# The last 64 tokens of every batch as a ninth 512-token block of the MLP beside the attention

## The chip, the cores and the metric

The kernel runs on one core of a Trainium2 chip. The metric is the device time of one execution in microseconds (us); lower is better. The kernel before has a median of 1210.61 us over three runs (1206.44 to 1210.83). Engines are named as in the profile: PE is TensorE (matrix products and transposes), PEld its weight loads, DVE is VectorE, ACT is ScalarE, POOL is GpSimd, SP is the engine that issues most DMAs.

## The reference: attention, then a gated MLP

Eight batches of 8 heads, 576 tokens, head size 64. A token of 64-token block i sees all tokens of blocks up to i. The attention's output, reordered to 4608 tokens of 512 features, goes through a gated MLP with 1536 hidden features:

```python
scores = scale * np.matmul(q, k.transpose(0, 1, 3, 2))
mask = block_i >= block_j
scores = np.where(mask, scores, -1000000000.0)
attn = softmax(scores)                       # exp, sum and division, written out in the reference
x = (attn @ v).transpose(0, 2, 1, 3).reshape(B * S, H * D)
...
gate = 1.0 / (1.0 + np.exp(-(x @ w_gate)))   # w_gate, w_val: 512 x 1536
val = x @ w_val
return (gate * val @ w_out).astype(np.float32)
```

The MLP's weights arrive as 64-bit floats and are converted in the kernel.

## The kernel before, in words

**Products.** A number of a product is split into a high and a low part, both in the reduced type float32r, and each product is made of three matmuls: high by high, high by low, low by high. The 1536 hidden features are 12 blocks f of 128 columns. Stage one, beside the attention, does the first four (F1 = 4); stage two, behind it, does the other eight in two groups of four, over six blocks of 768 tokens each, by a seven-product scheme on 2 by 2 blocks (`unit`, products in L834 with 384 columns, `out_block` at L892).

**Attention.** 32 pairs p of heads, four to a batch. `attend(p)` gives steps: scores and softmax of the four 128-token row blocks ("s": PE scores, DVE row maximum at L372, ACT exp at L375), the 64-token tail ("t"), transposes of the probabilities (L250, copied out by ACT at L350), and the product with v ("AV", in L247) of the pair before. AV's result is scaled by DVE (L486) into `xT`; `finish` (L491) writes its high part (ACT, L493) and low part (POOL, L496) into `XH`, `XL` of the batch, and a copy to the DRAM tensor `xT_d`. All attention steps on PSUM go through a pool of three two-bank tiles (`two_banks`, L254); a step waits until the tile that was used three steps ago is read out.

**The MLP of stage one.** `mlp1(b, bank)` (L556) is a generator that issues one matmul per step. For each f and each half of a batch (TA = 288 tokens), `hidden` (L121) makes 12 matmuls of 288 columns for gate and 12 for value; `glu` (L141) takes the tanh (ACT), multiplies (DVE, L147), writes the high part (ACT, L152) and the low part (POOL, for the last batch DVE, L153). That is 192 hidden matmuls a batch. The first 512 tokens lie in `hH`, `hL`; the last 64 in one half of `hHt`, `hLt`, which two batches share. Then `out_mm` (L130) makes 12 matmuls of 512 columns for each 128 tokens: four tiles for an even batch, five for an odd one, whose fifth is the 64 + 64 last tokens of both batches. ACT evicts them (L584) and writes them to `part_d`. While attention runs, stage one has two banks of its own (`mbank`); behind it, `bank` hands out halves of the two-bank tiles.

**What sets the order.** The step lists FIRST (pairs 0 to 6), TURN (7) and REST (8 to 31) give each attention step a number of ticks, 12 a pair. At AV of pair 4b + 4 the matmuls of `mlp1(b)` are added to `left`, and a rate is set so that KEEP of them are left when the next batch comes (L783, L784):

```python
left += F1 * 48 * NC // 4 + 3 * F1 * (5 if pb % 2 else 4)
rate = (left - KEEP[pb > 0]) / (4 * TICKS)
```

So a tick deals 5 or 5.25 matmuls, in batch 0 3.9, in batch 1 5.7. Scores and AV are ordered behind the matmuls dealt so far; a dealt matmul may move forward by up to three ticks (AHEAD). What is left, and all of batch 7, follows behind the attention (`run(mlp)`, L918). Beyond these constraints a scheduler fixes each engine's order at compile time by its own simulation.

**The transition.** Behind the attention DVE converts the first weights of stage two (`sums_gv`, `split_gv`: W00 and W01 in advance, then W10, W11 and `wo2`). The SBUF pools of stage two lie over those of stage one: in order from the end that is freed first, `x0` (features of the even batches), `w1` (gate and value weights of stage one, f = 0 first), `x1` (odd batches) and `m1` (all else of stage one). A tile of stage two is written when the tiles under it have been read for the last time.

Of the kernel before, what the change touches and what calls it, by code (L numbers as in the profile page):

```python
# [40 lines left out]
def attn_glu_kernel(ctx: ExitStack, tc: tile.TileContext, q, k, v, w_gate, w_val, w_out, out):  # L41
# [88 lines left out]
    def out_mm(ps, hH, hL, wo, nf, t):  # L130
        n = 3 * nf
        i = 0
        for f in range(nf):
            for lh, rh in ((hH, wo[:, f, 0]), (hL, wo[:, f, 0]), (hH, wo[:, f, 1])):
                mm = nc.tensor.matmul(ps, lhsT=lh[:, f, t * P:(t + 1) * P], rhs=rh, start=(i == 0), stop=(i == n - 1))  # L135
                i += 1
                yield mm.ins
# [3 lines left out]
    def glu(pool, pg, pv, dst, n, lower):  # L141
# [9 lines left out]
        for cols, hH, hL in dst:  # L151
            nc.scalar.copy(out=hH, in_=h2[:, cols])  # L152
            lower.tensor_sub(out=hL, in0=h2[:, cols], in1=hH.bitcast(F32))  # L153
# [7 lines left out]
    with ExitStack() as s2:  # L161
# [14 lines left out]
        def x_tiles(b):  # L176

            i = b % 2
            if i not in X:
                X[i] = [(xp1 if i else xp0).tile([P, NC, S], F32R, name=f"X{e}{i}") for e in "HL"]  # L180
            return X[i]
# [75 lines left out]
        spare = []  # L257

        def bank():
            if not spare:  # L260
                t = two_banks()
                spare.extend((t[:, 1], t[:, 0]))
            return spare.pop()
# [72 lines left out]
        def attend(p):  # L336
# [154 lines left out]
            def finish():  # L491
                XH, XL = x_tiles(b)
                nc.scalar.copy(out=XH[:, hp], in_=xT)  # L493
                nc.scalar.dma_start(
                    out=xT_d[b, hp * P:(hp + 1) * P, :], in_=xT)
                nc.gpsimd.tensor_sub(out=XL[:, hp], in0=xT, in1=XH[:, hp].bitcast(F32))  # L496
# [58 lines left out]

        def mlp1(b, bank):  # L556
            if not H1:
                H1.extend(mp.tile([P, F1, n], F32R, name=x) for n, x in ((512, "hH"), (512, "hL"), (P, "hHt"), (P, "hLt")))
            hH, hL, hHt, hLt = H1
            XH, XL = x_tiles(b)  # L560
            lo = 64 * (b % 2)
            if b == B - 1:
                ahead.extend(first_sums)
            for f in range(F1):
                convert_until(0, 2 * f + 2)
                for sub in range(2):
                    r = slice(sub * TA, (sub + 1) * TA)
                    pg = bank()
                    yield from hidden(pg[:, :TA], wg[f], XH[:, :, r], XL[:, :, r])
                    pv = bank()  # L570
                    yield from hidden(pv[:, :TA], wv[f], XH[:, :, r], XL[:, :, r])
                    if sub == 0:
                        dst = [(slice(0, TA), hH[:, f, :TA], hL[:, f, :TA])]
                    else:
                        dst = [(slice(0, 512 - TA), hH[:, f, TA:], hL[:, f, TA:]),
                               (slice(512 - TA, TA), hHt[:, f, lo:lo + 64], hLt[:, f, lo:lo + 64])]
                    glu(mp, pg, pv, dst, TA, nc.vector if b == B - 1 else nc.gpsimd)
            convert_until(1, F1)
            wo = W_out[0]
            for t in range(5 if b % 2 else 4):  # L580
                po = bank()
                yield from out_mm(po, *((hH, hL, wo, F1, t) if t < 4 else (hHt, hLt, wo, F1, 0)))
                ost = mp.tile([P, DM], F32, name="ost", bufs=2)
                nc.scalar.mul(out=ost, in_=po, mul=0.5)  # L584
                if t < 4:
                    r = b * S + t * P
                    nc.scalar.dma_start(out=part_d[r:r + P, :], in_=ost)
                else:
                    for j in range(2):
                        r = (b - 1 + j) * S + 512  # L590
                        nc.scalar.dma_start(out=part_d[r:r + 64, :], in_=ost[64 * j:64 * j + 64, :])

# [172 lines left out]
        for p in range(n + 1):  # L771
# [4 lines left out]
            for what, places in (FIRST if p < N_FIRST else TURN if p == N_FIRST else REST):  # L776
                if what.startswith(("AV", "TR")):
                    if prev:
                        prev(what.lower() if what == "AV" else what.lower()[:2] + what[2:])
                    if prev and what == "AV" and pairs[p - 1][1] == NP - 1:  # L780
                        pb = pairs[p - 1][0]
                        mlp = itertools.chain(mlp, mlp1(pb, mbank if p < n else bank))
                        left += F1 * 48 * NC // 4 + 3 * F1 * (5 if pb % 2 else 4)  # L783
# [134 lines left out]
        run(mlp)  # L918
        s1.close()
# [105 lines left out]
```

## Time and profile before

| | |
|---|---|
| median of three runs | 1210.61 us |
| the profiled execution | 1211.92 us, its span 1210.1 us |
| PE busy | 1167.7 us, 96% |
| DVE, ACT, POOL busy | 770.4, 627.7, 332.6 us |
| attention and stage one | up to about 641 us |
| stage two | from about 641 us |

A row of a group names line, engine, operation, output and inputs, shape and count; behind the bar stand busy time, the mean of one, and the engine's idle time ahead of them with what ended it. A row of the timeline starts with the start and the duration in us, and has idle time ahead of it in brackets. Matmuls are pipelined: one takes longer than the distance to the next, so the cost of a row of matmuls is read from start to start.

### The profile page before, as it was taken

Reading aid. Unit: us, or ns where it says so; the run is one execution under the profiler, and the core shown is the slowest. Engines: PE = TensorE matmul, PEld = TensorE weight load, DVE = VectorE, ACT = ScalarE, POOL = GpSimd, SP = SyncE. Lnnn points to the kernel's source line nnn. Section 1 sums busy time; section 2 is a strip of 40 time slices with the busy share of each in tenths; the row PEclk is TensorE's granted clock in tenths of the full one; section 3 lists DMA queues with packets and bytes.
Section 4 is the critical chain, followed back from the end, with each engine's and each line's share of the span. In section 5 each row is a group of like instructions: output and inputs, shape, how many; then the busy total and the mean of one; then the engine's idle time right before and its main releaser. Section 6 shows DMA issues by size and latency. Waiting matters only on the chain.

```text
span 1210.1 us, 20754 instructions
## 1 busy us (share of the span) xinstructions
PE 1167.7 (96%) x7421; PEld 1025.6 (85%) x7421; DVE 770.4 (64%) x1447; ACT 627.7 (52%) x1459; POOL 332.6 (27%) x411
## 2 busy tenths in 40 slices
PE   6989899999999999999999999999999999999996
PEld 3557789888888988888789889999999999998895
DVE  5678945356454545544899976866866655755743
ACT  6776857576676666666444453453454432422420
POOL 0123223133231331322101223123122153262331
PEclk8999999999999999999999999999999999999998
DMA  8664343543544443444243335235287154164153
GB/s 179 168 150 98 97 114 74 118 87 78 118 88 105 99 102 83 98 111 120 91 129 115 106 135 200 72 129 200 59 300 288 59 179 165 55 198 155 55 157 105
DMA packets 249112, 152.52 MB, mean 126 GB/s; under 512 B 189489, under 2 KB 209969, under 8 KB 248369
## 3 DMA queue, kind: packets, MB, share of 16 engines
q1 hardware_dynamic: 237952, 132.02, 39.5%
q10 hardware_dynamic: 11056, 19.17, 4.5%
q8 instruction: 58, 0.95, 0.3%
q14 instruction: 46, 0.37, 0.1%
HBM read 103.81 MB, written 47.33 MB: 125 GB/s over the span
## 4 chain that ended last, share of the span: by engine, by line
PE 73%; DVE 12%; DMA 6%; ACT 3%; POOL 2%; issue 2%; SPq 1%; POOLq 0%; DVEq 0%; ACTq 0%
PE b L834 19%; PE m L126 13%; PE bank L247 13%; PE m L892 9%; PE m L135 6%; PE bank L250 5%; PE b L892 5%; DMA pr<-part_d 3%; DVE XL L724 2%; POOL pr L907 1%; ACT P L375 1%; DMA XB<-xT_d 1%; DVE nm L372 1%; PE m L250 1%; PE bank L126 1%
## 5 line engine op out<-in xcount | busy, mean ns | idle before, releaser
L834 PE MATMUL b<-XH,w 128*128 128x384 f32 x1344 | 352.3, 337 | 5.0 <-DVE v L870 2.5
L834 PEld LDWEIGHTS b<-XH,w 128*128 128x128 f32 x1344 | 244.9, 188 | 12.4 <-DVE v L870 5.3
L834 PE MATMUL b<-XL,w 128*128 128x384 f32 x672 | 225.2, 336 | 0.0
L375 ACT ACTIVATE P<-bank,nm 128x512 f32<-128x512 f32 (+3 forms) x256 | 133.5, 538 | 69.7 <-DVE nm L372 59.0
L834 PEld LDWEIGHTS b<-XL,w 128*128 128x128 f32 x672 | 126.6, 188 | 1.3
L892 PE MATMUL m<-wo,hH 128*128 128x512 f32 x384 | 124.9, 391 | 0.0
L372 DVE TENSOR_REDUCE nm<-bank 128x2 f32<-128x1024 f32 (+3 forms) x128 | 105.0, 820 | 29.4 <-ACT P L375 26.8
L350 ACT COPY G<-bank 128x768 f32<-128x768 f32 (+3 forms) x140 | 93.2, 696 | 29.6 <-PE bank L250 26.2
L126 PE MATMUL m<-XH,wv 128*128 128x288 f32 x448 | 104.2, 304 | 1.7 <-DVE h L147 1.7
L126 PE MATMUL m<-XH,wg 128*128 128x288 f32 x448 | 104.2, 303 | 0.0
L247 PE MATMUL bank<-G,VS 128*64 128x320 f32 (+4 forms) x896 | 98.2, 361 | 0.0
L153 POOL TENSOR_TENSOR hL<-h,hH 128x288 fp32r<-128x288 f32 (+1 forms) x56 | 42.4, 757 | 199.6 <-ACT hH L152 190.7
L907 POOL TENSOR_TENSOR pr<-pr,pr 128x512 f32<-128x512 f32 x36 | 48.0, 1333 | 162.1 <-DMA pr<-part_d 139.5
L247 PEld LDWEIGHTS bank<-G,VS 128*64 128x64 f32 x896 | 55.9, 137 | 36.9 <-issue 3.5
L723 ACT CAST XH<-XB 128x1536 fp32r<-128x1536 f32 (+2 forms) x72 | 66.1, 938 | 34.6 <-DVE XB L721 25.1
L892 PEld LDWEIGHTS m<-wo,hH 128*128 128x128 f32 x384 | 71.9, 188 | 13.7
L857 ACT ACTIVATE g<-g 128x384 f32<-128x384 f32 x72 | 37.4, 524 | 81.6 <-DVE g L870 61.1
L724 DVE TENSOR_TENSOR XL<-XB,XH 128x1536 fp32r<-128x1536 f32 (+2 forms) x72 | 77.8, 1089 | 0.9 <-ACT XH L723 0.4
L126 PEld LDWEIGHTS m<-XH,wv 128*128 128x128 f32 x448 | 74.7, 188 | 4.0 <-DVE h L147 1.9
L392 DVE MEMSET bank<- 64x128 f32 x64 | 10.6, 165 | 105.8 <-PE bank L247 105.2
L126 PEld LDWEIGHTS m<-XH,wg 128*128 128x128 f32 x448 | 74.9, 188 | 3.2 <-issue 1.8
L250 PE MATMUL bank<-ident,P 128*128 128x128 f32 x560 | 75.4, 273 | 0.8 <-DVE rT L419 0.7
(179 smaller groups left out, 2488.4 us busy)
## 6 DMA issues: line engine op xcount, KB each, us to landing
pr<-part_d SPq DMA_DIRECT2D x72, 256.0 KB
xT_d<-xT ACTq DMA_DIRECT2D x32, 288.0 KB
XB<-xT_d SPq DMA_DIRECT2D x16, 576.0 KB
part_d<-ost SPq DMA_DIRECT2D x36, 256.0 KB
out_dram<-ost SPq DMA_DIRECT2D x36, 256.0 KB
VS<-in_v_dram SPq DMA_DIRECT2D x64, 128.0 KB
part_d<-ost ACTq DMA_DIRECT2D x32, 256.0 KB
rqk<-in_k_dram SPq DMA_DIRECT2D x108, 72.0 KB
```

Of the source, the lines that this page charges most:

```text
L126: mm = nc.tensor.matmul(ps, lhsT=lh, rhs=rh, start=(i == 0), stop=(i == n - 1))
L135: mm = nc.tensor.matmul(ps, lhsT=lh[:, f, t * P:(t + 1) * P], rhs=rh, start=(i == 0), stop=(i == n - 1))
L247: pe_last[:] = [nc.tensor.matmul(*args, **kw).ins]
L250: pe_last[:] = [nc.tensor.transpose(*args).ins]
L350: mark("ACT", nc.scalar.copy(out=dst, in_=src))
L372: mark("DVE", nc.vector.tensor_reduce(out=nm[:, c0:c0 + 2], in_=ps[:, :, c:c + n], axis=AX.X, op=ALU.max, negate=True))
L375: mark("ACT", nc.scalar.activation(out=Pi[:, h], in_=ps[:, h, c:c + n], func=AF.Exp, bias=nm[:, c0 + h:c0 + h + 1], accum_out=sm[:, 5 * h ...
L723: nc.scalar.copy(out=XO[j][0][:, a:b], in_=x)
L724: sub = nc.vector.tensor_sub(out=XO[j][1][:, a:b], in0=x, in1=XO[j][0][:, a:b].bitcast(F32))
L834: mm = nc.tensor.matmul(ps, lhsT=lh, rhs=rh, start=(first and k == 0), stop=(k == n - 1), skip_group_check=not first)
L892: mm = nc.tensor.matmul(po[t], lhsT=lh[:, f, t * P:(t + 1) * P], rhs=rh, start=(half == 0 and i == 0), stop=(half == 1 and i == 5))
L907: nc.gpsimd.tensor_add(out=pr[0], in0=pr[0], in1=pr[1])
```

## The change

Stage one takes 512 tokens of a batch in one product of 512 columns: 24 hidden matmuls per f, 96 a batch, and 48 for the output. The last 64 tokens of the eight batches become a ninth block, `mlp1(8)`, which runs behind batch 7, so behind the attention. Its features are made by `tail_x`: four DMAs read the last 64 tokens of batches 0 to 6 from `xT_d` into the low tile of the even batches, ACT rounds the high part, POOL subtracts, and POOL copies those of batch 7 from the odd batches' tiles. The even batches' tiles now lie in `x1` and the odd ones' in `x0`. `hHt` and `hLt` are gone, the tiles of `glu` are 512 wide. Behind the attention, `bank` alternates between halves of two-bank tiles and the two banks of stage one, the output is made two tiles at a time, with the last f of both at the end, and DVE makes the low parts for both last blocks. The ninth block's output is written by POOL's DMA queue. `left` counts 96 + 48 a batch; KEEP stays.

```diff
--- before.py
+++ after.py
@@ -127,13 +127,11 @@
                 i += 1
                 yield mm.ins
-    def out_mm(ps, hH, hL, wo, nf, t):
-        n = 3 * nf
-        i = 0
-        for f in range(nf):
-            for lh, rh in ((hH, wo[:, f, 0]), (hL, wo[:, f, 0]), (hH, wo[:, f, 1])):
-                mm = nc.tensor.matmul(ps, lhsT=lh[:, f, t * P:(t + 1) * P], rhs=rh, start=(i == 0), stop=(i == n - 1))
-                i += 1
+    def out_mm(ps, hH, hL, wo, t, fs):
+        for f in fs:
+            for i, (lh, rh) in enumerate(((hH, wo[:, f, 0]), (hL, wo[:, f, 0]), (hH, wo[:, f, 1]))):
+                mm = nc.tensor.matmul(ps, lhsT=lh[:, f, t * P:(t + 1) * P], rhs=rh, start=(f == i == 0),
+                                      stop=(f == F1 - 1 and i == 2))
                 yield mm.ins
     ahead = []
@@ -148,9 +146,9 @@
         for ins in ahead:
             behind(mul.ins, ins)
         ahead.clear()
-        for cols, hH, hL in dst:
-            nc.scalar.copy(out=hH, in_=h2[:, cols])
-            lower.tensor_sub(out=hL, in0=h2[:, cols], in1=hH.bitcast(F32))
+        hH, hL = dst
+        nc.scalar.copy(out=hH, in_=h2)
+        lower.tensor_sub(out=hL, in0=h2, in1=hH.bitcast(F32))
     def run(gen):
         for _ in gen:
@@ -177,7 +175,7 @@
             i = b % 2
             if i not in X:
-                X[i] = [(xp1 if i else xp0).tile([P, NC, S], F32R, name=f"X{e}{i}") for e in "HL"]
+                X[i] = [(xp0 if i else xp1).tile([P, NC, S], F32R, name=f"X{e}{i}") for e in "HL"]
             return X[i]
@@ -254,13 +252,11 @@
         def two_banks():
             return ps_a.tile([P, 2, 512], F32, name="bank")
-        spare = []
+        turns = itertools.cycle((1, 1, 0))
         def bank():
-            if not spare:
-                t = two_banks()
-                spare.extend((t[:, 1], t[:, 0]))
-            return spare.pop()
+            return two_banks()[:, 0] if next(turns) else mbank()
         def mbank():
             return ps_m.tile([P, 512], F32, name="m")
@@ -490,7 +486,9 @@
             def finish():
                 XH, XL = x_tiles(b)
-                nc.scalar.copy(out=XH[:, hp], in_=xT)
+                cut = nc.scalar.copy(out=XH[:, hp], in_=xT)
+                if p == len(pairs) - 1:
+                    mark("ACT", cut)
                 nc.scalar.dma_start(
                     out=xT_d[b, hp * P:(hp + 1) * P, :], in_=xT)
                 nc.gpsimd.tensor_sub(out=XL[:, hp], in0=xT, in1=XH[:, hp].bitcast(F32))
@@ -553,49 +551,60 @@
         H1 = []
+        NM = 4 * P
+        def tail_x():
+            XH, XL = x_tiles(B)
+            XH1, XL1 = x_tiles(B - 1)
+            done = (B - 1) * D
+            for c in range(NC):
+                src = xT_d[0:B - 1, c * P:(c + 1) * P, NM:S].rearrange("b p s -> p b s")
+                nc.sync.dma_start(out=XL[:, c, :done].rearrange("p (b s) -> p b s", s=D).bitcast(F32), in_=src)
+            x = XL[:, :, :done].bitcast(F32)
+            cut = nc.scalar.copy(out=XH[:, :, :done], in_=x)
+            behind(cut.ins, last["ACT"])
+            nc.gpsimd.tensor_sub(out=XL[:, :, :done], in0=x, in1=XH[:, :, :done].bitcast(F32))
+            for dst, src in ((XH, XH1), (XL, XL1)):
+                nc.gpsimd.tensor_copy(out=dst[:, :, done:NM], in_=src[:, :, NM:S])
         def mlp1(b, bank):
             if not H1:
-                H1.extend(mp.tile([P, F1, n], F32R, name=x) for n, x in ((512, "hH"), (512, "hL"), (P, "hHt"), (P, "hLt")))
-            hH, hL, hHt, hLt = H1
+                H1.extend(mp.tile([P, F1, NM], F32R, name=x) for x in ("hH", "hL"))
+            hH, hL = H1
+            if b == B:
+                tail_x()
             XH, XL = x_tiles(b)
-            lo = 64 * (b % 2)
             if b == B - 1:
                 ahead.extend(first_sums)
             for f in range(F1):
                 convert_until(0, 2 * f + 2)
-                for sub in range(2):
-                    r = slice(sub * TA, (sub + 1) * TA)
-                    pg = bank()
-                    yield from hidden(pg[:, :TA], wg[f], XH[:, :, r], XL[:, :, r])
-                    pv = bank()
-                    yield from hidden(pv[:, :TA], wv[f], XH[:, :, r], XL[:, :, r])
-                    if sub == 0:
-                        dst = [(slice(0, TA), hH[:, f, :TA], hL[:, f, :TA])]
-                    else:
-                        dst = [(slice(0, 512 - TA), hH[:, f, TA:], hL[:, f, TA:]),
-                               (slice(512 - TA, TA), hHt[:, f, lo:lo + 64], hLt[:, f, lo:lo + 64])]
-                    glu(mp, pg, pv, dst, TA, nc.vector if b == B - 1 else nc.gpsimd)
+                pg = bank()
+                yield from hidden(pg, wg[f], XH[:, :, :NM], XL[:, :, :NM])
+                pv = bank()
+                yield from hidden(pv, wv[f], XH[:, :, :NM], XL[:, :, :NM])
+                glu(mp, pg, pv, (hH[:, f], hL[:, f]), NM, nc.vector if b >= B - 1 else nc.gpsimd)
             convert_until(1, F1)
             wo = W_out[0]
-            for t in range(5 if b % 2 else 4):
-                po = bank()
-                yield from out_mm(po, *((hH, hL, wo, F1, t) if t < 4 else (hHt, hLt, wo, F1, 0)))
-                ost = mp.tile([P, DM], F32, name="ost", bufs=2)
-                nc.scalar.mul(out=ost, in_=po, mul=0.5)
-                if t < 4:
+            step = 2 if b >= B - 1 else 1
+            for t in range(4):
+                if t % step == 0:
+                    po = {u: bank() for u in range(t, t + step)}
+                    for fs in ((range(F1 - 1), range(F1 - 1, F1)) if step > 1 else ()):
+                        for u in po:
+                            yield from out_mm(po[u], hH, hL, wo, u, fs)
+                if step == 1:
+                    yield from out_mm(po[t], hH, hL, wo, t, range(F1))
+                ost = mp.tile([P, DM], F32, name="t" if b == B and t > 1 else "ost", bufs=2)
+                nc.scalar.mul(out=ost, in_=po[t], mul=0.5)
+                if b < B:
                     r = b * S + t * P
                     nc.scalar.dma_start(out=part_d[r:r + P, :], in_=ost)
                 else:
                     for j in range(2):
-                        r = (b - 1 + j) * S + 512
-                        nc.scalar.dma_start(out=part_d[r:r + 64, :], in_=ost[64 * j:64 * j + 64, :])
+                        r = (2 * t + j) * S + NM
+                        nc.gpsimd.dma_start(out=part_d[r:r + 64, :], in_=ost[64 * j:64 * j + 64, :])
         W_OF = {1: 0, 5: 1, 2: 2, 4: 3, 7: 4, 6: 5, 3: 6}
         X_OF = {1: 0, 7: 1, 2: 2, 3: 3, 5: 4, 6: 5, 4: 6}
@@ -780,7 +789,7 @@
                     if prev and what == "AV" and pairs[p - 1][1] == NP - 1:
                         pb = pairs[p - 1][0]
                         mlp = itertools.chain(mlp, mlp1(pb, mbank if p < n else bank))
-                        left += F1 * 48 * NC // 4 + 3 * F1 * (5 if pb % 2 else 4)
+                        left += F1 * 6 * NC + 3 * F1 * 4
                         rate = (left - KEEP[pb > 0]) / (4 * TICKS)
                 elif what in "kq":
                     next(pr, None)
@@ -916,6 +925,7 @@
             sums = sums_gv(*e, alone=done)
         x_split(early_x, sums)
         run(mlp)
+        run(mlp1(B, bank))
         s1.close()
         for u in units[1:]:
             wp[u] = pool(f"w{u[0]}{u[1]}")
```

## The prediction

> **What bounds the kernel now.** I read the page first (busy shares, slices), then the windows by stage, then the timeline of PE around the transition.
>
> ```profile
> span 1210.1 us, 20754 instructions
> PE 1167.7 (96%) x7421; PEld 1025.6 (85%) x7421; DVE 770.4 (64%) x1447; ACT 627.7 (52%) x1459; POOL 332.6 (27%) x411
> ...
> PE   6989899999999999999999999999999999999996
> ```
>
> PE is the bound nearly everywhere. The windows (busy us of PE, PEld, DVE, ACT, POOL, then granted clock, DMA share, GB/s) say where it is not:
>
> ```profile
> 74.60:144.73 70.13, 63.53 (x462) 49.53 (x463) 59.05 (x112) 48.98 (x130) 18.89 (x24) 1.00 0.46 111
> 144.73:570.50 425.77, 425.70 (x3307) 370.53 (x3307) 219.03 (x444) 279.12 (x740) 125.86 (x208) 1.00 0.43 99
> 588.60:641.70 53.10, 50.57 (x301) 45.59 (x300) 50.35 (x106) 22.66 (x45) 3.17 (x3) 1.00 0.36 120
> 641.70:671.50 29.80, 27.59 (x157) 26.63 (x155) 29.55 (x58) 16.78 (x29) 5.50 (x4) 0.99 0.34 106
> 671.50:707.50 36.00, 36.00 (x176) 33.03 (x177) 33.52 (x54) 14.48 (x27) 10.89 (x9) 0.96 0.41 140
> ```
>
> The second row is the attention from AV of pair 7, which is issued in pair 8, to that of pair 30: PE has no idle, DVE works half the time, ACT two thirds. The first row, where batch 0's MLP begins, has 6.6 us of PE idle beside a DVE busy for 84%. The third and fourth are the transition: DVE is busy 95% and 99%, PE loses 4.7 us. So in most of the attention a matmul saved is time saved; in the first row it mostly isn't; in the transition more PE work costs its own length less the idle that it fills.
>
> **The prices.** Rows of PE's timeline, the first and last of a run without a break. From 612.00 to 615.16 lie 24 matmuls of 288 columns: 131.7 ns each. From 626.28 to 632.65 lie 28 of 512 columns: 227.5 ns each.
>
> ```profile
> 612.00 0.29 PE L126 MATMUL bank<-XH,wg 128*128 128x288 f32 x1
> ...
> 615.16 0.30 PE L126 MATMUL bank<-XH,wg 128*128 128x288 f32 x1
> ...
> 626.28 0.39 PE L135 MATMUL bank<-wo,hH 128*128 128x512 f32 x1
> ...
> 632.65 0.39 PE L135 MATMUL bank<-wo,hL 128*128 128x512 f32 x1
> ```
>
> Between attention steps, 18 of 288 columns lie from 476.54 to 478.94 (133.3 ns), and runs of 10 and 12 of 512 in the chain take 232 and 228 ns; I take 230.
>
> ```profile
> 476.54 0.43 PE L126 MATMUL m<-XH,wg 128*128 128x288 f32 x2
> ...
> 478.94 0.43 PE L126 MATMUL m<-XH,wv 128*128 128x288 f32 x2
> ```
> ```profile
> 306.16 2.32 PE m L135 x10
> ...
> 437.99 2.74 PE m L135 x12
> ```
>
> The columns of the hidden products are the same before and after: 1536 x 288 = 864 x 512. 1536 matmuls cost 1536 x 0.1317 = 202.3 us, 864 cost 864 x 0.2275 = 196.6 us. So the wider product alone is worth 5.7 us of PE, no more. The Trainium skill ("TensorE: Matmul & The Clock Gate", Back-to-back issue gap) gives N/2.4 + 2.5 ns a matmul: 122.5 and 215.8 ns, by which it would be worth an estimated 1.7 us. The rows here lie above both, by 9 and 12 ns, and I go by them.
>
> **Part by part, stage by stage.**
>
> First, the stretch up to AV in pair 8. Batch 0 deals all but KEEP = 52 of its matmuls there: 188 of 288 columns before (188 x 0.1333 = 25.1 us), 92 of 512 after (21.2 us). PE has less to do by 3.9 us, beside a busy DVE. Bounds 0 and -3.9; the window's 6.6 us of idle says nearer to 0: **-0.5 us**.
>
> Second, pairs 8 to 31. From AV in pair 8 to AV in pair 32 there are 24 x 12 - 4 = 284 ticks (pair 32 deals none ahead of its AV). Before, 52 are left at both ends, so 1152 hidden and 324 output matmuls run: 1152 x 0.1333 + 324 x 0.230 = 153.6 + 74.5 = 228.1 us. After, the rates are 3.4 for batch 1 and 3 a tick for the others, 44 are left at the end, and 52 + 6 x 144 - 44 = 872 run, all of 512: 200.6 us. PE is the bound, so **-27.5 us**. Most of that is the last 64 tokens leaving.
>
> Third, behind the attention, up to stage two. Before: 4 + 192 hidden and 48 + 60 output matmuls, 196 x 0.1317 + 108 x 0.2275 = 50.4 us, in the window's 53.1. After: 44 left, batch 7's 144 and the ninth block's 144: 332 x 0.2275 = 75.5 us: **+25.1 us**.
>
> Fourth, idle of PE in the transition. These rows carry it: waits of 1.28, 1.24 and 2.02 us; 12 matmuls from 671.47 to 675.05 that take 3.58 us, where 12 of a steady run (16.50 us for 95) take 2.08; two hitches of 0.4 and 0.3 us against the 0.51 us that two such matmuls take at 641.84. Together 6.7 us.
>
> ```profile
> 619.80 0.40 PE L126 MATMUL bank<-XH,wg 128*128 128x288 f32 x1 [1.28 <-DVE h L147]
> ...
> 638.59 0.50 PE L135 MATMUL bank<-wo,hH 128*128 128x512 f32 x1 [1.24 <-ACT ost L584]
> ...
> 641.84 0.51 PE L834 MATMUL b<-XH,w 128*128 128x384 f32 x2
> ...
> 642.36 0.91 PE L834 MATMUL b<-XH,w 128*128 128x384 f32 x2
> ...
> 667.73 0.84 PE L834 MATMUL b<-XH,w 128*128 128x384 f32 x2
> ...
> 671.47 0.69 PE L834 MATMUL b<-XH,w 128*128 128x384 f32 x1 [2.02 <-DVE g L870]
> ...
> 675.05 0.40 PE L892 MATMUL m<-wo,hH 128*128 128x512 f32 x1
> ```
> ```profile
> 743.78 16.50 PE b L834 x95
> ```
>
> After, PE has 75.5 us of stage one in which DVE, whose list grows by one block's glu alone, gets ahead; `bank` then has five slots of one product each, so the first to be reused are two f behind, 11 us. I take 6.0 of the 6.7 as gone (bounds: none, and all): **-6.0 us**.
>
> What else is moved is hidden. The ninth block's features: four DMAs on SP, at worst behind the 15.10 us of weight loads below; the nearest landing of such a read is 7.42 us; ACT's cut of 1792 columns is 1.7 us by 1.48 for 1536; POOL's subtraction 4.7 us by 1511 ns for 576. That is 29 us against 332 - 144 = 188 matmuls, 42.8 us, ahead of the block. POOL, which gets this and eight output DMAs, sat idle for 62 us there. The cut waits in ACT's queue for the DMAs; behind it stand batch 7's tanh and casts, and PE misses those only when all five slots are full, 11 us later. The DMAs wait for the last hidden product of batch 6, and none of these is left behind the last AV (the 44 are output products).
>
> ```profile
> 583.77 15.10 SPq L643 DMA_DIRECT2D raw<-in_moe_w_val_dram  x4
> ```
> ```profile
> 568.45 7.42 DMA XB<-xT_d
> ```
> ```profile
> L496 POOL TENSOR_TENSOR XL<-xT,XH 128x576 fp32r<-128x576 f32 x32 | 48.4, 1511 | 58.0 <-ACT XH L493 56.1
> ...
> L723 ACT CAST XH<-XB 128x1536 fp32r<-128x1536 f32 x24 | 34.9, 1476 | 9.2 <-PE b L834 8.1 <-PE m L135 1.0
> ```
> ```profile
> 655.70 1.85 POOL L842 TENSOR_TENSOR hL<-t,hH 128x384 fp32r<-128x384 f32 x1 [62.23 <-ACT hH L841]
> ```
>
> The ninth block reads `w1` longer, and W10 and W11 lie over it. Before, DVE ends W10 and W11 from 634.76 and 649.19 on, 46 and 61 us behind the last AV (588.6).
>
> ```profile
> 634.76 2.10 DVE L679 TENSOR_TENSOR w<-cT,w 128x896 fp32r<-128x896 f32 x2 [1.85 <-ACT w L678]
> ...
> 649.19 2.10 DVE L679 TENSOR_TENSOR w<-cT,w 128x896 fp32r<-128x896 f32 x2 [0.22 <-ACT w L678]
> ```
>
> After, its hidden matmuls are over at 42.8 + 96 x 0.2275 = 64.6 us; if DVE waits for all of them, W10 is there at 67 and W11, 14 us behind as now, at 81. PE needs W10 at 75.5 + two units of 42 x 0.174 = 7.3 us, 90, and W11 at 97. Nothing waits. Stage two behind this is untouched.
>
> Sum: -0.5 - 27.5 + 25.1 - 6.0 = **-8.9 us**. The profiled execution took 1211.9 us, so 1203.0; the median shown is 1.3 us lower than that execution, so **1201.7 us**.
>
> **The rivals.**
>
> *The softmax chain becomes the bound (slower).* AV is ordered behind the matmuls dealt between scores and AV, 20 or 21 before, 12 after, and needs the bank that ACT's second exp group frees.
>
> ```profile
> 475.99 0.39 PE L247 MATMUL bank<-KQ 64*128 64x128 f32 x4
> ...
> 479.20 0.30 PE L247 MATMUL bank<-KH,QBH 128*128 128x288 f32 x1
> ...
> 480.08 1.30 PE L247 MATMUL bank<-G,VS 128*64 128x320 f32 x8
> ```
> ```profile
> 479.26 0.21 ACT L375 ACTIVATION_READ_ACCUMULATOR P<-bank,nm 128x1 f32 x1
> ```
> ```profile
> L584 ACT ACTIVATE ost<-m 128x512 f32<-128x512 f32 x31 | 18.8, 605 | 8.4 <-PE m L135 8.1
> ```
>
> Here the bank is free at 479.47 and AV starts at 480.08. After, from 476.30 (the scores' end): 12 x 0.230, 0.1 for the change of operands and the 0.88 of the tail's scores give 480.04, about the same, since 12 wide matmuls last as long as 20 narrow ones. But ACT's ops of glu, 512 wide, cost 0.6 us (the eviction's row). One ahead of that exp brings it to 480.08, two to 480.68: 0.64 us of wait in each of 24 pairs is 15.4 us, 1218.4 on the profiled execution, 1217.1 as a median. From 0.37 us a pair on the change gains nothing. For it: the margin of one op. Against: ACT's work per f falls (one tanh and one cut, where there were two and six), so two in one place should be rare. Chance 0.13.
>
> *The idle in the transition is not won back* (a wait for the space under W10, or SP held by a read of `part_d` rows that are now written last). Then the first three terms are left, -2.9 us: 1209.0, or 1207.7 as a median; no change. For it: DVE at 95 to 99% in two windows, and tiles that are freed later. Against: the margins of 23 and 16 us above. Chance 0.22.
>
> *Hidden products of 512 columns run worse than output products of 512.* At 4 ns more, the distance of the two 512 rates above (228 and 232), 864 x 0.004 = 3.5 us of the gain are lost: 1205.2. No row shows a hidden product of 512; weights and columns come from the same kinds of tile as the output's. Chance 0.1. The Trainium skill's rule above would leave out an estimated 4.0 us and come to much the same time.
>
> **How the numbers follow.** My forecast has 0.55. About 0.5%, 6 us, is what a measurement of this kernel can tell from no change: faster is below 1204.6, slower above 1216.7. The forecast's own range is 1196 (all idle and the whole 3.9 us won) to 1205. Faster: nearly all of the forecast and a little of the third and second rivals, 0.62; slower: most of the first, 0.11; the rest, 0.27, within. The range starts 1.7 us lower, at 1194 (872 matmuls at 228 instead of 230 ns), and ends at 1212, between the second rival and the first, which leaves out most of the first.
>
> **What would show it.** Right: AVs a steady 17.3 us apart (425.77 / 23 - 27.5 / 24), where the starts below are 16.8 and 20.6 us apart; hidden 512 products at 228 to 231 ns; stage two begins some 4 us earlier than at 641.5 and PE's idle up to the second k is under 1 us. Wrong: idle or a gap ahead of AV or the tail's scores with ACT exp as releaser; waits of PE for `w` or `XH` of the ninth block; L834's first rows later than 641.
>
> ```profile
> 244.28 2.86 PE bank L247 x28
> 261.05 2.86 PE bank L247 x28
> ...
> 442.44 2.86 PE bank L247 x28
> ...
> 463.06 2.86 PE bank L247 x28
> ```

## The result and the profile after

| | before | after |
|---|---|---|
| median | 1210.63 us (4 runs, 1206.44 to 1210.83) | 1195.19 us (4 runs, 1194.74 to 1197.00) |
| profiled execution, its span | 1211.92, 1210.1 us | 1194.74, 1193.0 us |

The ratio is 0.9883, with a 95% interval of 0.9860 to 0.9907: 15.4 us faster, where 8.9 were forecast. The 1195.2 us lie just below the forecast's own range (1196 to 1205) and inside the wider one (1194 to 1212). Both kernels were profiled a second time, so that a stage's difference can be held against how well it repeats. The stages are cut at rows of PE: start of AV in the step of pair 8, last matmul of the last AV, first product of stage two, last matmul.

| stage, us | before | before, second | after | after, second | change (first profiles) | forecast |
|---|---|---|---|---|---|---|
| up to AV in pair 8 | 144.7 | 145.9 | 140.7 | 140.8 | -4.0 | -0.5 |
| to the last AV | 443.7 | 443.5 | 414.2 | 414.3 | -29.5 | -27.5 |
| to stage two | 53.1 | 53.0 | 73.6 | 73.6 | +20.5 | +22.6 |
| stage two | 558.6 | 558.7 | 555.2 | 556.9 | -3.4 | -3.5 |
| sum | 1200.1 | 1201.1 | 1183.8 | 1185.6 | -16.3 | -8.9 |

The rest of the spans' 17.1 us, 0.8, lies behind the last matmul. (The 6.0 us of idle of the forecast are put where they lay: the waits of 1.28 and 1.24 us ahead of stage two, 25.1 - 2.5 = 22.6, and the other 3.5 in it.) The two middle stages repeat within 0.2 us, the outer two within 1.3 and 1.7. For the first stage two profiles show too little: six more kernels below, with the changed kernel's products up to there (`noswap` with the features in other tiles), reach AV in pair 8 at 140.1 to 142.8 us. The least distance from before, 144.7 to 142.8, is still more than the 0.5 of the forecast, but its size is known to some 2 us only.

First the page of the changed kernel: PE is a little busier in its share, with 672 matmuls fewer.

```profile
span 1193.0 us, 19280 instructions
PE 1160.0 (97%) x6749; PEld 976.8 (82%) x6749; DVE 774.3 (65%) x1415; ACT 619.7 (52%) x1372; POOL 320.4 (27%) x366
...
PE   6998999999999999999999999999999999999996
```

Then its windows by stage (busy us of PE, PEld, DVE, ACT, POOL, clock, DMA share, GB/s), which answer to the five of before.

```profile
74.60:140.70 66.10, 60.77 (x375) 40.80 (x375) 57.53 (x107) 46.45 (x117) 17.93 (x18) 1.00 0.49 118
```
```profile
140.70:549.84 409.14, 409.14 (x2788) 324.00 (x2787) 224.81 (x438) 275.95 (x687) 115.63 (x163) 1.00 0.44 104
554.93:628.50 73.57, 73.57 (x329) 60.76 (x326) 60.41 (x106) 28.27 (x43) 7.71 (x5) 1.00 0.28 94
628.50:658.00 29.50, 27.34 (x158) 26.99 (x156) 28.08 (x55) 16.95 (x29) 8.35 (x12) 0.99 0.40 125
658.00:694.00 36.00, 36.00 (x176) 33.03 (x177) 31.04 (x50) 12.57 (x24) 10.53 (x9) 0.96 0.49 166
```

PE has no idle at all from AV of pair 8 to stage two, 73.57 of 73.57 us behind the attention, where it had lost 2.5. DVE is busy 82% there instead of 95%. The start of stage two still has 2.2 us of idle, and DVE is still full there (28.08 of 29.50).

AV is now evenly spaced: its starts in PE's timeline lie 17.08 us apart from pair 12 to pair 31 (17.3 in the mean from pair 8 on, the forecast's figure), where they swung between 16.7 and 21.6.

```profile
231.08 2.93 PE L245 MATMUL bank<-G,VS 128*64 128x320 f32 x28
...
248.16 2.93 PE L245 MATMUL bank<-G,VS 128*64 128x320 f32 x28
...
265.24 2.93 PE L245 MATMUL bank<-G,VS 128*64 128x320 f32 x28
```

The hidden product of 512 columns, which no row of before showed: nine in 2.08 us in the attention, 231 ns each; behind it 12 in 2.72 us, 226.7 ns.

```profile
244.74 0.63 PE L126 MATMUL m<-XH,wg 128*128 128x512 f32 x2
...
246.82 0.62 PE L126 MATMUL m<-XH,wv 128*128 128x512 f32 x2
```
```profile
595.88 0.39 PE L126 MATMUL bank<-XH,wg 128*128 128x512 f32 x1
...
598.60 0.39 PE L126 MATMUL m<-XH,wg 128*128 128x512 f32 x1
```

The ninth block's features and the weights that lie over `w1`, in the timelines of ACT, POOL and DVE:

```profile
557.43 1.70 ACT L565 CAST XH<-XL 128x1792 fp32r<-128x1792 f32 x1 [0.64 <-DMA XL<-xT_d]
```
```profile
559.82 4.52 POOL L567 TENSOR_TENSOR XL<-XL,XH 128x1792 fp32r<-128x1792 f32 x1
```
```profile
618.52 2.09 DVE L688 TENSOR_TENSOR w<-cT,w 128x896 fp32r<-128x896 f32 x2
...
634.24 1.09 DVE L688 TENSOR_TENSOR w<-cT,w 128x896 fp32r<-128x896 f32 x1 [1.13 <-ACT w L687]
...
635.72 1.08 DVE L688 TENSOR_TENSOR w<-cT,w 128x896 fp32r<-128x896 f32 x1
...
649.10 1.20 DVE L702 TENSOR_TENSOR wo<-cT,wo 128x512 fp32r<-128x512 f32 x1
```

The features are ready at 564.3, and PE comes to the ninth block at 595.88, so they are hidden. W10 and W11 are done 65.7 and 81.9 us behind the last AV (554.93), against 67 and 81 in the forecast. PE waits for neither.

The start of stage two in PE's timeline, in the first and the second profile of the same changed kernel, and the rows of DVE ahead of the first:

```profile
657.90 0.69 PE L843 MATMUL b<-XH,w 128*128 128x384 f32 x1 [2.16 <-DVE g L879]
```
```profile
654.49 0.95 DVE L733 TENSOR_TENSOR XL<-XB,XH 128x768 fp32r<-128x768 f32 x1
...
656.42 0.95 DVE L733 TENSOR_TENSOR XL<-XB,XH 128x768 fp32r<-128x768 f32 x1
657.29 0.55 DVE L879 TENSOR_TENSOR g<-b,g 128x384 f32<-128x384 f32 x1
```
```profile
658.25 0.44 PE L843 MATMUL b<-XH,w 128*128 128x384 f32 x1 [2.38 <-DVE g L879]
```

So the wait of 2.02 us of before has stayed: PE needs a bank that the sum at 657.29 reads, and that sum stands in DVE's queue behind conversions of the output's weights and the low parts of the next features (L733). In the first profile the 12 matmuls behind the wait take 3.6 us (661.54 - 657.90), in the second 2.2.

Last, PE's waits from the first output of stage two to the end (us in total, times, longest), of before and of the changed kernel's second profile; the first profile of the changed kernel has none.

```profile
PE b L834 <- DVE v L870: 2.5, 6, 1.1
```
```profile
PE b L843 <- ACT ost L910: 1.7, 1, 1.7
PE b L843 <- DVE g L879: 0.2, 1, 0.2
```

### The profile page after: what moved, and what is told of

Read it like the earlier page. It is cut to its first block, busy times and chain, and to the rows that moved or that the text cites. A ratio compares the mean times of both kernels' runs of the same rounds, so it can differ in the third digit from the quotient of the medians.

```text
span 1193.0 us, 19280 instructions
## 1 busy us (share of the span) xinstructions
PE 1160.0 (97%) x6749; PEld 976.8 (82%) x6749; DVE 774.3 (65%) x1415; ACT 619.7 (52%) x1372; POOL 320.4 (27%) x366
## 4 chain that ended last, share of the span: by engine, by line
PE 83%; DVE 7%; ACT 3%; DMA 3%; issue 1%; POOL 1%; SPq 1%; POOLq 0%; DVEq 0%; ACTq 0%
PE b L843 23%; PE bank L245 13%; PE m L126 13%; PE m L901 10%; PE m L133 8%; PE bank L248 5%; PE b L901 5%; PE bank L126 3%; ACT P L371 2%; DMA pr<-part_d 1%; PE m L248 1%; DVE XL L733 1%; PE bank L133 1%; POOL pr L916 1%; ACT G L346 1%
## 5 line engine op out<-in xcount | busy, mean ns | idle before, releaser
L901 PE MATMUL m<-wo,hH 128*128 128x512 f32 x384 | 124.9, 391 | 0.0
L133 PE MATMUL m<-wo,hH 128*128 128x512 f32 x256 | 84.9, 397 | 0.0
L126 PE MATMUL m<-XH,wv 128*128 128x512 f32 x240 | 82.4, 401 | 0.0
L126 PE MATMUL m<-XH,wg 128*128 128x512 f32 x240 | 82.2, 399 | 0.0
L733 DVE TENSOR_TENSOR XL<-XB,XH 128x1536 fp32r<-128x1536 f32 (+2 forms) x72 | 77.7, 1085 | 0.1
L901 PE MATMUL m<-wo,hL 128*128 128x512 f32 x192 | 75.2, 392 | 0.0
L248 PEld LDWEIGHTS bank<-ident,P 128*128 128x128 f32 x560 | 66.0, 141 | 11.3 <-ACT G L346 0.7
```

The costliest lines, as they stand in the source:

```text
L126: mm = nc.tensor.matmul(ps, lhsT=lh, rhs=rh, start=(i == 0), stop=(i == n - 1))
L248: pe_last[:] = [nc.tensor.transpose(*args).ins]
L733: sub = nc.vector.tensor_sub(out=XO[j][1][:, a:b], in0=x, in1=XO[j][0][:, a:b].bitcast(F32))
L901: mm = nc.tensor.matmul(po[t], lhsT=lh[:, f, t * P:(t + 1) * P], rhs=rh, start=(half == 0 and i == 0), stop=(half == 1 and i == 5))
```

## The experiments

Theory: the gain is the output work and the rows of PE that leave the attention, where PE has no idle. Rivals: the wide product in itself; the rules on banks, output order and tiles that came with it. All kernels but `keep80` and the two repeats are edits of the changed kernel, whose 1195.2 us they are held against; times are medians, ratios are to the kernel before, run beside them. Its medians there were 1208.3 to 1209.5, beside the changed kernel 1210.6, so a distance of some 2 us from 1195.2 says nothing by itself.

**The width alone.** Each hidden product as two halves of 256 columns, dealt together:

```python
ops = [(w[:, c, a], x[:, c]) for c in range(NC) for a, x in ((0, xH), (0, xL), (1, xH))]
for h in range(2):
    r = slice(256 * h, 256 * h + 256)
    for i, (lh, rh) in enumerate(ops):
        mm = nc.tensor.matmul(ps[:, r], lhsT=lh, rhs=rh[:, r], start=(i == 0), stop=(i == n - 1))
        if i % 2:
            yield mm.ins
```

> The changed kernel with each hidden product made as two halves of 256 columns into the same bank; blocks, glu, dealing by ticks and the ninth block stay. Theory (the matmul's fixed cost is the gain): a matmul takes its columns plus about 12 ns, so 256 columns take 118 ns, 1728 of them 204 us where 864 of 512 take 196.6: about 8 us slower than the changed kernel, some 1203 us. Rival (the gain is in the longer product groups and in fewer, larger glu operations, that is in waits): no change, within 1 us. A third outcome: weight loads bound the narrow products, then they take over 130 ns and it is over 20 us slower.

1214.96 us, ratio 1.0050 [1.0032, 1.0068]: about 20 us more than the changed kernel, and more than either expectation. Two rows of PE, 24 matmuls apart:

```profile
607.16 0.28 PE L127 MATMUL bank<-XH,wg 128*128 128x256 f32 x1
...
610.03 0.28 PE L127 MATMUL bank<-XH,wv 128*128 128x256 f32 x1
```

2.87 us, 120 ns each, so two halves cost 12.5 ns more than one whole, and 864 of them 10.8 us. The stages show +10.0 up to the last AV, +3.7 behind it, -1.1 ahead and +7.0 in stage two. The first two hold the price of the halves: 771 products of the changed kernel lie in these stages, 9.6 of the 13.7 us. PE shows no wait in either, so the other 4 us are slower matmuls, and why is open. The last comes with another order of stage two (below), with more waits there, and was in no expectation.

**The ninth block or not.** Products of 512, but the tails of two batches as a 128-token block beside the attention; the features stay in the tiles of before, and `h2` has one buffer:

```diff
+                for f in range(F1):
+                    pt = bank()
+                    yield from hidden(pt[:, :P], wg[f], *XT)
+                    yield from hidden(pt[:, P:2 * P], wv[f], *XT)
...
-        run(mlp1(B, bank))
```

> The 512-column products without the ninth block: the last 64 tokens of each two batches make a 128-token block of their own behind the odd batch's output, beside the attention, with 128-column hidden products (feature tiles laid out as before, one buffer for the product of glu instead of two). Theory (it pays only because the tails are gathered into one 512-column block): 384 narrow products at 65 ns (128 columns plus 12 ns) to 109 ns (the distance of the 128-column transposes) cost 25 to 42 us where the ninth block's hidden products cost 21.8, and the idle behind the attention stays: 1203 to 1225 us, nearer to the upper end. Rival (512 columns alone are the gain): as fast as the changed kernel, about 1195.

1227.2 us, ratio 1.0149 [1.0119, 1.0179], slightly above the theory's upper end. The rows say why a narrow tail is dear:

```profile
644.36 0.28 PE L126 MATMUL bank<-XTH,wv 128*128 128x128 f32 x1
...
645.59 0.27 PE L126 MATMUL bank<-XTH,wv 128*128 128x128 f32 x1
```

Eleven in 1.23 us: 112 ns for 128 columns, half the price of 512. Four such blocks are 384 x 0.112 + 48 x 0.230 = 54.0 us, the ninth block is 144 x 0.2275 = 32.8. The attention and what lies behind it took 24.7 us longer (454.6 and 57.9), 3.0 of it in waits of PE. So gathering all eight tails is worth some 21 us, and the change needs both its parts: wide products with tails in pairs lose 17.7 us to the kernel before. Not all of these 17.7 need be the tails' doing: this kernel also has one buffer for `h2`, and 8.4 us of its distance to the changed kernel lie ahead of pair 8 and in stage two.

**Banks and the order of the output.** Both rules of before behind the attention, then each alone:

```diff
-            return two_banks()[:, 0] if next(turns) else mbank()
+            if not spare:
+                t = two_banks()
+                spare.extend((t[:, 1], t[:, 0]))
+            return spare.pop()
...
-            step = 2 if b >= B - 1 else 1
+            step = 1
```

> The changed kernel with the old handing out of banks behind the attention (both halves of a two-bank tile, three tiles) and with the output one tile at a time. Theory (the ninth block's mass of work covers the waits): at most 1 us slower. Rival (the waits of 1.3 and 1.2 us behind the attention went because of the five slots and the late last f): 2.5 us slower or more, with waits of PE for DVE's product of glu and for ACT's eviction.

> The changed kernel with only the old handing-out of banks (a list of the two halves of a two-bank tile, none of stage one's two banks); the output still two tiles at a time. The run with both old rules was 7 us slower than the change: 5.9 us of it between the last AV and stage two, 1 us in stage two. Theory: the banks carry it, since three two-bank tiles that come free only as pairs make PE wait for the evictions: 5 to 6 us longer behind the attention than the change's 73.6 us, about 1201 us in all. Rival: the order of the output's products carries it, the banks nothing: 73.6 us behind the attention and 1195 to 1196 us in all.

> The changed kernel with only the output of the last two blocks made one tile at a time, as in the rest; the banks as in the change. Theory (the banks carry the 7 us): at most 1 us longer behind the attention, 1195 to 1197 us. Rival (the order of the output carries it): the first output products of a block wait for the last f's high and low parts, one gap of 2 to 3 us for each of the two blocks, so 4 to 6 us longer behind the attention and 1200 to 1202 us.

Both rules: 1202.11, ratio 0.9946 [0.9929, 0.9963], 79.5 us behind the attention instead of 73.6. The old banks alone: 1200.86, 0.9941 [0.9926, 0.9956], 75.8 us. The old order alone: 1196.71, 0.9908 [0.9892, 0.9925], 73.6 us. PE's waits behind the attention up to stage two, of the first:

```profile
587.21 0.50 PE L133 MATMUL bank<-wo,hL 128*128 128x512 f32 x1 [1.14 <-DVE hL L151]
...
588.27 0.50 PE L133 MATMUL bank<-wo,hH 128*128 128x512 f32 x1 [0.34 <-DVE h L145]
...
601.66 0.50 PE L126 MATMUL bank<-XH,wg 128*128 128x512 f32 x1 [0.71 <-DVE h L145]
```

The first expectation's theory (at most 1 us) fell: with both rules PE waits 3.4 us there, and these rows are most of it. The banks carry most of the time, as the second expected of the sum, but not in the place it named: only 2.2 us lie behind the attention. Stage two is longer by 3.6 us against the changed kernel's first profile and by 2.0 against its second, so how much of that the banks caused is open. The order alone costs too little to be told from the change. The two together cost more behind the attention (5.9 us) than each alone.

**The tiles of the features.** Even batches back in `x0`, odd ones in `x1`, so that the ninth block holds the space that is freed first:

```diff
-                X[i] = [(xp0 if i else xp1).tile([P, NC, S], F32R, name=f"X{e}{i}") for e in "HL"]
+                X[i] = [(xp1 if i else xp0).tile([P, NC, S], F32R, name=f"X{e}{i}") for e in "HL"]
```

> The changed kernel with the feature tiles laid out as before: even batches in x0, odd ones in x1, so that the ninth block reads x0, over which W01 lies. Theory (DVE's list behind the attention is set by the tiles that the ninth block frees): W01 is split only when the block's hidden products end, about 64 us behind the last AV instead of about 36, W10 and W11 some 14 us later each than now; PE, which needs W11 at about 97 us, then waits: 8 to 14 us slower, 1203 to 1209. Rival (the margins hold all of it): no change.

1207.65, ratio 0.9991 [0.9978, 1.0004]: 12.5 us lost, as the theory had it. Stage two begins at 629.3, nearly as without the edit (628.5), but its first output comes 41.0 us later instead of 33.0, behind W11 and `wo2` (timelines of DVE and PE):

```profile
655.72 2.08 DVE L688 TENSOR_TENSOR w<-cT,w 128x896 fp32r<-128x896 f32 x2
```
```profile
670.26 0.79 PE L901 MATMUL m<-wo,hH 128*128 128x512 f32 x1 [3.72 <-ACT wo L701]
```

W11 is done 102 us behind the last AV, not 82. Of the loss 8.0 us lie up to the first output; in the rest of the stage PE waits 7.0 us, the 3.7 of this row among them. The forecast's second rival (tiles that come free too late) was a real mechanism; the swap of two pools, which the forecast passed over in a clause, kept it away.

**The wait at the start of stage two.** The sums of the second features on POOL, then the low parts of the output's weights on POOL:

```diff
-            x_sums(XB, nc.vector, sums_after)
+            x_sums(XB, nc.gpsimd)
```

> The changed kernel with the three sums for each half of the second block's features made by POOL instead of DVE. In the changed kernel PE still waits 2.2 us for DVE in stage two's first block and then runs at about half speed for 12 matmuls (3.8 us where 2.1 is normal), while DVE is busy for 34.1 of 35.5 us there. Theory (DVE's list is the bound in that stretch): 3.3 us less of DVE work takes the wait away, 3 to 4 us faster than the changed kernel, about 1191.5. Rival (the wait comes from the order of DVE's list, not from its length): no change.

```diff
-            nc.vector.tensor_sub(out=dst[:, 1], in0=T[:, :4 * P], in1=dst[:, 0].bitcast(F32))
+            nc.gpsimd.tensor_sub(out=dst[:, 1], in0=T[:, :4 * P], in1=dst[:, 0].bitcast(F32))
```

> The changed kernel with the low parts of stage two's output weights made by POOL (idle there) instead of DVE. The wait of 2.16 us at the start of stage two is for a DVE sum that starts at 657.29, and DVE is busy 34.08 of 35.5 us there, 1.9 of them with two of these subtractions. Theory: the length of DVE's list keeps the wait; it falls to about 0.3 us, the slow matmuls behind it (1.7 us too long) go too, and the first output of stage two comes 2 to 3 us earlier than the 33.0 us behind its start: about 1192.5 us. Rival: the order of DVE's list keeps it (the features of the next tokens stand ahead of the sum): the wait stays at 2 to 3 us and the time within 1 us of the change.

The first: 1195.56, ratio 0.9887 [0.9865, 0.9908], no change. The second: 1198.93, 0.9905 [0.9880, 0.9931], not faster. PE's waits of the two in their timelines:

```profile
659.29 0.44 PE L843 MATMUL b<-XH,w 128*128 128x384 f32 x1 [2.86 <-DVE v L879]
```
```profile
657.78 0.44 PE L843 MATMUL b<-XH,w 128*128 128x384 f32 x1 [1.16 <-DVE v L876]
...
660.32 0.44 PE L843 MATMUL b<-XH,w 128*128 128x384 f32 x1 [1.22 <-DVE g L879]
...
662.46 0.44 PE L843 MATMUL b<-XH,w 128*128 128x384 f32 x1 [0.81 <-DVE v L879]
```

The wait stays, or falls into three of 3.2 us in all. Taking these operations from DVE doesn't remove it. DVE is nearly as busy without them up to the first output of stage two (30.98 of 32.43 us and 31.74 of 33.17), since other conversions move up, so its list ahead of the sum did not get shorter as the theory meant. The length of the list is therefore not ruled out, and that another order would remove the wait was not tried.

**The front.** The kernel before with `KEEP = (80, 32)`, so that 28 matmuls fewer (3.7 us) are dealt ahead of AV in pair 8:

> The kernel before with 80 instead of 52 matmuls of batch 0 kept back, so that 160 of 288 columns are dealt before AV in pair 8 instead of 188, that is 21.3 us of PE instead of 25.1, as much as in the changed kernel. Theory (a matmul dealt there lengthens the stretch by its own time although PE shows idle in it): AV in pair 8 starts at 140.7 instead of 144.7, and as the 28 come back in the stretch where PE is the bound, the total stays within 1 us. Rival (DVE paces that stretch, as the prediction had it): AV in pair 8 at about 144.2, the total 3 us slower.

1210.93, ratio 1.0012 [0.9995, 1.0028]. AV of pair 8 starts at 141.8, 2.9 us earlier: nearer the theory (140.7) than the rival (144.2). The AV ahead of batch 0's MLP and that of pair 8, in PE's timeline:

```profile
70.80 0.49 PE L247 MATMUL bank<-G,VS 128*64 128x320 f32 x2
...
141.80 0.49 PE L247 MATMUL bank<-G,VS 128*64 128x320 f32 x2
```

The first of the two starts at 71.60 in the kernel before, so 0.8 of the 2.9 us arise ahead of the edit's first effect. By the rows 24 matmuls fewer (180 to 156, 3.2 us) run in the front, and between the two AVs it is 2.1 us shorter than in the first profile of before and 2.6 shorter than in the second. The attention took 3.8 us more, since the matmuls were only moved. The total, 1.4 us up with an interval from 0.6 down to 3.4 up, decides nothing. So matmuls saved in the front count for some two thirds or more, in spite of its idle.

**How near the next bound is.** One of the three output matmuls of stage one instead of three, with `KEEP = (20, 12)`; the output's low parts are left out.

> The changed kernel with one of the three matmuls of each output product of stage one (high by high); the two others are left out, so 16 instead of 48 a block, and the numbers kept back are scaled. It asks how far the next bound of a pair lies. If PE stays the bound, a pair takes 17.08 - 8 x 0.231 = 15.2 us and the total falls by 288 x 0.2275 = 66 us. If the softmax chain (DVE's maximum, ACT's exp, the bank) takes over, a pair stays above 16 us and PE shows waits for ACT ahead of AV or of the tail's scores.

1167.15, ratio 0.9642 [0.9614, 0.9670]: 28 us less, where 288 matmuls less are 66 us. AVs come 15.5 to 18.0 us apart, 16.2 in the mean. PE's longest waits over the whole kernel (us in total, times, longest), and behind them the one of the changed kernel that answers to the first:

```profile
PE bank L244 <- ACT P L370: 9.5, 14, 1.9
PE m L133 <- ACT hH L149: 7.2, 5, 1.5
```
```profile
PE bank L245 <- ACT P L371: 6.1, 7, 2.5
```

Of the first row 6.4 us lie ahead of AV in pair 8, where the changed kernel has its 6.1, so they are not new. From there to the last AV PE waits 13.0 us where the changed kernel waits for nothing: 7.2 for the high part of glu's result, 3.1 for exp and 1.5 for ACT's copy of the transposed probabilities. Another 9.6 us of waits, for glu, lie behind the attention, and stage two is 3.8 to 5.5 us longer. So much of what is taken out turns into waits, more of them for glu than for the softmax chain that the expectation named. The next pace of a pair, with these products, lies about 1 us below the changed kernel's 17.08.

**The two kernels once more.**

> The kernel before, unchanged, a second profiled execution, to see how far a stage's length repeats. Theory: each stage repeats within 1 us (144.7 up to AV of pair 8's step, 443.7 to the last AV, 53.1 to stage two, 558.6 in it), so that the change's -4.0, -29.5, +20.5 and -3.4 us belong to the change. Rival: the stretch up to pair 8, which reads most from DRAM, and stage two vary by 2 us and more between executions of the same program, and the first profile of before was on the long side in both (it was 1.3 us above the median): about 142.5 and 557.

> The changed kernel, unchanged, a second profiled execution, for the same question. Theory: each stage repeats within 1 us (140.7, 414.2, 73.6, 555.2). Rival: the middle two repeat, the first and the last vary by 2 us and more: up to 143 and 557, as the run with the output weights on POOL had it (142.8 and 556.8) with the same code up to pair 8.

1212.71 and 1196.92 us, one execution each; the stages stand in the table above. Neither theory nor rival holds as a whole: the middle repeats within 0.2 us and the front's difference stands (-5.1 in the second pair of profiles), while stage two's is -3.4 in one pair and -1.8 in the other.

## Why the prediction was right, and where not

**The side and the mechanism were right.** PE without idle in the attention, the tail's work out of it, 144 wide matmuls behind it: the two large terms came out at -29.5 and +20.5 for -27.5 and +22.6. The steps for ACT (forecast 1.7 us, measured 1.70), POOL (4.7, measured 4.52), the DMAs (features ready 9.4 us behind the last AV, 29 allowed for), W10 and W11 (67 and 81, measured 65.7 and 81.9) held. Of the signs that the forecast gave for being right, evenly spaced AVs and 227 to 231 ns a product came true; PE's idle up to the second k, forecast under 1 us, is 2.2.

**"Bounds 0 and -3.9; the window's 6.6 us of idle says nearer to 0: -0.5 us."** This term was mis-sized: it measured -4.0 (-5.1 in the second profiles). The step from "a window has idle" to "a saved matmul isn't time saved" failed. In 74.60 to AV of pair 8 PE's busy time fell by 2.8 us (63.53 to 60.77) and its idle by 1.3 (6.60 to 5.33). Both were forecast otherwise: the saving of work as 3.9 us (by the rows 180 hidden matmuls ran there before and 93 after, for 188 and 92, which is 2.5 us), and the idle as what swallows it. My reading is that the idle sits at places of its own, and that the matmuls ahead of it move the chain that waits. `keep80` agrees with other matmuls, 2.1 to 2.6 us for 3.2 of work; why the idle fell as well is not shown.

**The attention, -27.5, measured -29.5.** By counts, PE made 1167 hidden and 324 output matmuls before, 880 in all after: 1167 x 0.1333 + 324 x 0.230 - 880 x 0.231 = 26.8 us. Of the remaining 2.7 us, 2.4 are idle in pair 32 of before that the forecast did not list, since its window ended at 570.50:

```profile
578.53 0.85 PE L250 MATMUL bank<-ident,P 128*128 128x128 f32 x6 [0.74 <-DVE rT L419]
...
583.20 0.40 PE L126 MATMUL m<-XH,wv 128*128 128x288 f32 x1 [1.67 <-DVE h L147]
```

**Behind the attention, +22.6, measured +20.5.** The forecast had 332 matmuls there; 323 were left, as nine more ran ahead of the last AV: 323 x 0.2275 = 73.5 us, the 73.57 of the window. Those nine are in the 880 above.

**"I take 6.0 of the 6.7 as gone".** The two waits ahead of stage two went (2.5 us), as argued: more time and independent banks. `oldspare` and `oldbank` show that the banks are needed for that. The reason did not reach the other 3.5 us. "Nothing waits" was true of W10 and W11, but the wait at the start of stage two is for a sum behind DVE's later conversions, which begin when W11 is done and moved along with it. Stage two's beginning, up to its first output, got shorter by 0.6 us only (33.6 to 33.0); in the second profiles by 1.7 (33.5 to 31.8), because there the matmuls behind the wait were not slow. That stage two as a whole came out at -3.4 for -3.5 is therefore luck: the other 2.8 us lie behind the first output, where the forecast expected nothing, and in the second pair of profiles they are missing.

**"Stage two behind this is untouched."** Its code is, its compile-time order is not. In each later step the order of PE's units and output products is one of two (`pairtails`, `oldbank` and `thin` have some steps of each). The kernels that keep mainly to the order of before (before, `keep80`, `noswap`, `split256`, `oldbank`, and `poolwo`) each have four to six waits for the DVE sum `v` behind the first output, 1.4 to 2.5 us together; those with the other order (the changed kernel, `poolsums`, `oldspare`, `onestep`) have 0.3 us of them or none. In the first pair of profiles this accounts for the gain there: from the first output to the last matmul 524.7 us became 521.8, and the 2.5 us of waits are gone. But the times don't separate the two orders. This part takes 523.2 to 527.5 us in the profiles with the first and 521.8 to 524.7 in those with the second, whose longest is the changed kernel's second profile, with 1.9 us of other waits. So these waits go with the order; whether the order makes the stage shorter is not shown. That it comes out by the scheduler's simulation of what stands ahead is my reading; no kernel had the order alone changed.

**The rivals.** The softmax chain did not become the bound: PE has 409.14 of 409.14 us busy, and `thin` puts the next pace about 1 us a pair lower. The second rival was about half true: of its 6.0 us, 2.5 were won back ahead of stage two and 0.6 (1.7 in the second profiles) in its beginning. The third was false: hidden products of 512 run at 227 and 231 ns like the output's.

## What to carry to other kernels

Idle in a window doesn't mean that work taken out beside it is worth nothing: ask on which side of the waits the work stands, or move some of it and measure. Count the waits of every stage up to the very edge of the window, and when a conversion moves, follow its engine's queue past the pieces that were named, to whoever waits for the work behind them. A change of some matmuls can alter the compile-time order of code it doesn't touch, and with it the waits there (2.5 us of one kind came or went here), so compare kernels stage by stage and each with a second profile.

## What the runs showed of the hardware

The distance of two matmuls in float32r was 112, 120, 132 and 227 ns at 128, 256, 288 and 512 columns. Between the last two lie 0.425 ns a column; the line through them gives 118 ns at 256, close to the row, but 64 at 128, where the row has 112. A narrow tail costs half a full block.

After a wait of some 2 us PE may run at about half its pace for a while: 3.6 us for 12 matmuls in one profile of the changed kernel, with a granted clock of 0.56 over them, and 2.2 us in its second, with 1.00, behind a longer wait (2.38 us). `onestep` was spared too (a wait of 2.42 us, 2.2 us for 12), while the kernel before was hit in both its profiles (2.02 and 2.01 us, 3.6 and 3.5 us for 12). The windows from the start of stage two to its first output, of the one and of the other, have the granted clock behind the five engines:

```profile
628.50:661.50 33.00, 30.84 (x169) 30.49 (x168) 31.58 (x59) 17.89 (x30) 8.35 (x12) 0.95 0.36 112
```
```profile
628.70:660.50 31.80, 29.42 (x170) 29.03 (x169) 30.19 (x59) 17.82 (x30) 8.30 (x12) 1.00 0.38 116
```

The two stretches differ by 1.2 us: 1.4 less for these 12 matmuls, 0.2 more of wait. The Trainium skill ("TensorE: Matmul & The Clock Gate", Part 1: The HAM clock gate) says that the clock is gated by activity in a free-running window of about 3.4 us. That the same place is hit in one execution and spared in another agrees with a free-running window; the waits that were hit here, 2.01 to 2.16 us, are shorter than the window it gives.
